# Pieces of the last store, an earlier register load, and three steps moved in a fused attention and MLP kernel

## The chip, the cores and the metric

The kernel runs on one core of one Trainium2 chip. The metric is device time in microseconds for one launch. The core's engines have queues of their own and are named as in the profile: PE (TensorE, matmul), PEld (its weight loads), DVE (VectorE), ACT (ScalarE), POOL (GpSimd) and SP (SyncE, which here does little but issue DMAs and wait). Each engine takes its instructions in program order and waits for others by semaphores.

## The reference

Routing attention with 4 batches, 8 heads, 768 tokens and a head width of 64, followed by an MLP with an ELU between its two products, on 3072 tokens of width 512 with 2048 hidden units:

```python
q_assign = np.argmax(np.einsum('bhsd,hcd->bhsc', q_n, c_n), axis=-1)
k_assign = np.argmax(np.einsum('bhsd,hcd->bhsc', k_n, c_n), axis=-1)
mask = q_assign[:, :, :, None] == k_assign[:, :, None, :]
scores = np.where(mask, scale * np.matmul(q, k.transpose(0, 1, 3, 2)), -1000000000.0)
attn = softmax(scores)
x = np.matmul(attn, v)          # (B,H,S,D) -> (B*S, H*D)
h = x @ w_in
g = np.where(h > 0.0, h, np.exp(np.minimum(h, 0.0)) - 1.0)
out = (g @ w_out).astype(np.float32)
```

Each of q_n, k_n and c_n is its tensor divided by its rows' norms; a query sees only the keys of its own cluster, out of 16 for each head.

## The kernel before

**Attention** (0 to about 331 us) goes through 32 blocks, one for each batch, half of the queries (384) and pair of heads. `slot(n)` works on block n: it multiplies the last block's probabilities with v (`values`, L548), then makes the scores of block n in six steps (`plain`, L510, `masked`, L523), with the exponential on ACT (L532). In odd slots row sums of two blocks come first (`row_sums`, L568). DVE adds up probabilities (L535, L540, L541), and turns raw q and k, loaded in 32 x 32 pieces, into the layout of the matmuls (L715 and near it). POOL later multiplies the results with the reciprocals of the row sums (`scale_x`, L604), two multiplications for two blocks; the reciprocals stand in `r_of` and `e_of`, which are columns of `sums_w`.

All loads of q, k, v and the weights are issued by SP, in program order. `slot_first` is block 0. At its end it asks for the first pair of heads of batch 1's k, for weights, for the second half of q of batch 0 (16 DMAs), and for the second pair of k of batch 1 (four DMAs, `load_k(1, 1)`). `slot(1)` then asks for v of block 2 (`load_v(2)`), `slot(2)` for v of block 3, and so on. There are two buffers for v and two for raw k; the second k buffer is read by the transpose in `slot(3)`.

**The MLP** (331 us to the end) takes the tokens in six groups of 512. Both of its products use a Winograd form of Strassen's scheme, with seven products in place of eight, so there are sums of blocks of x, of the weights and of the hidden values beside the matmuls. Group 0 differs: its first product runs in four calls of `unit(0, u, ...)`, u from 0 to 3, beside the unpacking of the last weights and the sums of blocks of `w_out`.

One `unit` multiplies in the order b1 (a11), b4 (s1), b2 (s2), b1 (a12), b3 (s3), b2 (s4), b3 (a22), each `block_product` being eight matmul instructions of L797. ACT, POOL and DVE make the ELU of four parts: c11 after the fourth product, c12, c22 and c21 later. `elu_exp` is an exponential on ACT (L810) and then a clamp on POOL (L811); `elu` finishes on DVE (L814). L853 and L863 are DVE additions into the banks b2 and b4, which the product with s4, and the parts c22 and after, need. What is left of a unit when its matmuls are issued (`rest_of`: clamp of c21, elu of c12, c22 and c21, a subtraction at L880, and the last of three sums of weights for the next unit, L780 with its DMA) goes into the list `behind`, which `flush_all` issues after the first product of the next unit.

`fill()` is called at four places of a unit. In group 0 it takes one step from the list of weight work. By unit 3 the steps left are three sums of halves of `w_out` (`weight_sum`): 1 (L387), 2 (L389) and 3 (L391), each one DVE addition or subtraction with 2048 elements in a partition; sum 0 (L385) is the last step of unit 2. Sum 2 writes columns of `sums_w` where `r_of` and `e_of` lie. The two multiplications of the last two blocks (`scale_x(last_n - 1, ...)`, `scale_x(last_n, ...)`) are issued between unit 2 and unit 3; the tokens that they write are those of the last group.

`second_product_first` is the second product of group 0: M1 (a11 with b11), M2 (a12 with b21) and M3, then Strassen's form in `chain`. b11 is made of all c11 parts and b21 of all c21 parts; of each of its eight matmul pairs the last two read the part of unit 3.

**The end.** `chain` also does the last group. Its last unit multiplies m6, m2, m7, m3, m4, each eight matmul instructions of L1087, and `take` adds the results into `o_all`: after m2 and before it, columns 0 to 384 of tile 0 and 0 to 256 of tile 1 are there; after m7 and m3 the rest of tile 1; after m4 the last 128 columns of tile 0. The stores of tiles 2 and 3 are issued by SP some products before; those of tiles 1 and 0 by ACT, after m3 and after m4, with 256 KB each. When all is done each engine loads the verdict (`values_load`, L56: an integer in `c["go"]`, made at about 400 us), and branches on it (L57) over `general_path`, which is another form of the whole kernel for inputs that the main form can't do.

Of the kernel before, what the change touches and what calls it, by code (L numbers as in the profile page):

```python
# [30 lines left out]
@with_exitstack  # L31
def kernel(
    ctx: ExitStack,
    tc: tile.TileContext,
    q: bass.AP,
    k: bass.AP,
    v: bass.AP,
    centroids: bass.AP,
    moe_w_in: bass.AP,
    moe_w_out: bass.AP,  # L40
    out: bass.AP,
):
    nc = tc.nc
    ctx.enter_context(nc.allow_non_contiguous_dma(reason="token and weight layouts"))
    keep = ctx.enter_context(tc.tile_pool(name="keep", bufs=1))
    DM, DF = moe_w_in.shape
    c = {
        "ident": keep.tile([P, P], F32, name="ident"),
        "cen": keep.tile([P, q.shape[3]], F32, name="cen"),
        "w_in": keep.tile([P, DM // P, DF], F32, name="w_in"),  # L50
        "w_out": keep.tile([P, DF // P, DM], F32, name="w_out"),
        "ok": keep.tile([P, 4], F32, name="ok"),
        "go": keep.tile([1, 1], I32, name="go"),
    }
    main_path(tc, c, q, k, v, centroids, moe_w_in, moe_w_out, out)
    good = nc.values_load(c["go"][0:1, 0:1], min_val=0, max_val=P)  # L56
    with tc.If(good < P):  # L57
        general_path(tc, c, q, k, v, moe_w_in, moe_w_out, out)


# [1 line left out]
def main_path(ctx, tc, c, q, k, v, centroids, moe_w_in, moe_w_out, out):  # L62
# [569 lines left out]
    def slot_first():  # L632

        for _ in range(6):
            nc.tensor.matmul(
                o_bank, lhsT=blank, rhs=blank[:, 0:1].to_broadcast([P, 512]), start=True, stop=True
            )
        for pr in range(NPR):
            turned(qT[0][pr], first_q[pr], 0)
        nc.tensor.transpose(o_bank[:, :P], work[:, : 2 * D], ident)  # L640
        nc.vector.tensor_copy(cT, o_bank[:, :P])
        clusters_q(0, 0, d_bank)()
        for pr in range(NPR):
            turned(kT[0][pr][:, :CUT], first_k[pr], 0)
        turned(kT[0][0][:, CUT:], first_k[0], CUT // P)
        told = [clusters_k(0, 0, o_bank)]
        flush()
        for pr in range(1, NPR):
            turned(kT[0][pr][:, CUT:], first_k[pr], CUT // P)
        mask_q(0, 0, range(1, 2))  # L650
        first = ring()
        plain(0, 0, first)
        told.append(clusters_k(0, 1, d_bank))
        told[0]()
        flush()
        told[1]()
        load_k(1, 0)
        ask()
        load_q(0, 1)
        load_k(1, 1)  # L660
        for kt in range(NT):
            s = ring() if kt else first
            if kt:
                plain(0, kt, s)
            masked(0, kt, s)
            exponential(kt, s)
            if kt == 2:
                flush()
            elif kt == 3:
                sums_begin()  # L670


    def slot(n):
        b, at = n // NB, n % NB
        more = b + 1 < B
        sums_of = n - 2 if n > 1 and n % 2 else None
        pair_done = n - 4 if n >= 4 and n % 2 == 0 else None
        if sums_of is not None:
            row_sums(sums_of)
            take_sums(sums_of)  # L680
        flush(powers)
        if n > 0:
            values(n - 1)
        told = None
        if at == (1 if b else 3):
            told = clusters_q(b, 1, d_bank)
        elif at == 5 and more:
            told = clusters_q(b + 1, 0, d_bank)
        elif at in (6, 7) and more:
            told = clusters_k(b + 1, at - 6, d_bank)  # L690
        if n > 0:
            sums_end(n - 1)
        if pair_done is not None:
            nc.gpsimd.tensor_copy(mark, summed[(n - 1) % 2][:, :1])
            scale_x(n - 4, r_of)
            scale_x(n - 3, e_of)
        if n > 0:
            take_values(n - 1)
        if told is not None:
            told()  # L700
        if sums_of is not None:
            reciprocals(sums_of)
            spread(sums_of)

        if n + 1 < len(blocks):
            load_v(n + 1)
        if at == 0 and b:
            nc.vector.transpose(qT_all[1], raw_q_all)
        if at == 1 and b and more:
            load_q(b + 1, 0)  # L710
        if at == 0 and more:
            load_k(b + 1, 0)
            load_k(b + 1, 1)
        elif 2 <= at < 6 and more:
            nc.vector.transpose(kT[(b + 1) % 2][at - 2], raw_k[at % 2])  # L715
            if n == 2:
                nc.vector.transpose(qT_all[1], raw_q_all)
                load_q(1, 0)
            if at < 4:
                load_k(b + 1, at)  # L720
            elif at == 4:
                nc.vector.transpose(qT_all[0], raw_q_all)
                load_q(b + 1, 1)
        weigh(n)

        for kt in range(NT):
            s = ring()
            plain(n, kt, s)
            masked(n, kt, s)
            exponential(kt, s)  # L730
            if kt == 3:
                sums_begin()
        flush(later)
# [92 lines left out]
    def unit(k_, u, after_second=None, fill=None):  # L826

        fill = fill or (lambda: None)
        x11, t3, x21, x22 = x_parts(k_)
        t1, t2, t4 = x_s  # L830
        a11, a12, s1, a22 = w_parts(u)
        s2, s3, s4 = (w_tmp[:, m] for m in range(3))
        b1, b2, b3, b4 = sets[(k_ + u) % 2]
        m5, u3 = stage[:, 0], stage[:, 1]
        low, high = slice(2 * u, 2 * u + 2), slice(FC // 2 + 2 * u, FC // 2 + 2 * u + 2)
        c11, c12 = g[:, low, :QS], g[:, low, QS:]
        c21, c22 = g[:, high, :QS], g[:, high, QS:]

        block_product(b1, a11, x11, True)
        nc.scalar.copy(b2, b1)  # L840
        flush_all()
        yield
        block_product(b4, s1, t1, True)
        nc.scalar.copy(m5, b4)
        if after_second is not None:
            after_second()
        if k_ == 1 and u == 3:
            for _ in slots_w:
                fetch()
        yield  # L850
        block_product(b2, s2, t2, False)
        nc.scalar.copy(b3, b2)
        nc.vector.tensor_tensor(b2, b2, m5, op=Alu.add)  # L853
        fill()
        fill()
        if u < 3:
            w_step(k_, u + 1, 0)
        block_product(b1, a12, x21, False)
        elu_exp(c11, b1)
        block_product(b3, s3, t3, False)  # L860
        nc.scalar.copy(u3, b3)
        elu(c11, b1)
        nc.vector.tensor_tensor(b4, b4, u3, op=Alu.add)  # L863
        if k_ > 0:
            for t in {2: ("t1",), 3: ("t2", "t3", "t4")}.get(u, ()):
                t_step(0, t)
        fill()
        block_product(b2, s4, x22, False)
        if u < 3:
            w_step(k_, u + 1, 1)  # L870
        elu_exp(c12, b2)
        elu_exp(c22, b4)
        fill()
        block_product(b3, a22, t4, False)

        def rest_of():
            elu_exp(c21, b3)
            elu(c12, b2)
            elu(c22, b4)
            nc.vector.tensor_tensor(c12, c22, c12, op=Alu.subtract)  # L880
            elu(c21, b3)
            if u < 3:
                w_step(k_, u + 1, 2)

        behind.append(rest_of)
# [367 lines left out]
    def chain(units):  # L1253
# [6 lines left out]
        for i, u in enumerate(units):  # L1260
# [14 lines left out]
            u.product("m2")  # L1275
            u.take(0)
            u.note("m2")
            if nxt:
                seven_first(nxt)
            u.product("m7")  # L1280
# [9 lines left out]
            u.product("m3")  # L1290
            u.take(1)
            if ending:
                store_tile(u.k_, 1, nc.scalar)
            u.product("m4")
            if nxt:
                nxt.t("t4")
            u.note("m4")
        if ending:
            u.take(2)
            store_tile(u.k_, 0, nc.scalar)  # L1300
        elif u.of == "in":
            u.take(2)
        else:
# [116 lines left out]
        elif m == "M4":  # L1420
            store(k_, 0)

    def store_tile(k_, tile_, by):
        n = 4 * k_ + tile_
        at, t = n // HT, n % HT
        by.dma_start(
            out[at * HS : (at + 1) * HS].rearrange("(p t) m -> p t m", t=HT)[:, t],
            o_all[:, tile_],
        )

    def store(k_, tiles):
# [121 lines left out]
    def early_on():  # L1553
        while steps:
            weigh_step(*steps.pop(0))
            flush()

    blanks(0)
    for u in range(4):
        if u == 1:  # L1560
            blanks(1)
        run(unit(0, u, finish_attention if u == 0 else None, fill_weights))
        if u == 1:
            findings()
        elif u == 2:
            scale_x(last_n - 1, r_of)
            scale_x(last_n, e_of)
    second_product_first(early_on)

    table = table_rest()  # L1570
# [276 lines left out]
```

## Time and profile before

Three runs took 888.82, 889.41 and 889.57 us; the median is 889.41.

| | before |
|---|---|
| profiled execution | 889.5 us |
| its span, first to last instruction | 887.7 us |
| granted TensorE clock | 0.998 |
| PE busy | 876.6 us, 99% |
| DVE busy | 710.7 us, 80% |
| ACT busy | 447.0 us, 50% |
| POOL busy | 227.3 us, 26% |
| DMA, mean over the span | 164 GB/s |

The profile is one execution. In a timeline a line has the start and the time of an instruction or of several alike in us, the engine, the line of the code, what is written and read, and in brackets the idle time of the engine before it with what ended that. A matmul in f32 is two instructions of the trace. Ends of matmuls are modelled, so distances between starts are the surer measure. Shares of busy time are means over stages that differ: attention, the first group and the others.

### The profile page before, as it was taken

To read this page: it belongs to the slowest core of one execution; us is meant where nothing else is said; L and a number is where in the kernel's file an instruction comes from. 1 tells how busy PE (TensorE), PEld (TensorE's weight loads), DVE (VectorE), ACT (ScalarE), POOL (GpSimd) and SP (SyncE) were. 2 spreads that over 40 slices of the span, in tenths; PEclk is the share of its full clock that TensorE was granted. 3 is DMA by queue.
4 is the path that set the end of the run, shared out by engine and by line. 5 is a ranking of instruction groups with operands and counts; after the bars stand their busy time and mean duration, and the time that the engine had idled before them with its cause. 6 is when DMAs were issued, how large, how long until landed. Compare 5 with 4: busy or idle time off the path is not lost.

```text
span 887.7 us, 17035 instructions
## 1 busy us (share of the span) xinstructions
PE 876.6 (99%) x6437; PEld 677.6 (76%) x6441; DVE 710.7 (80%) x1041; ACT 447.0 (50%) x853; POOL 227.3 (26%) x293
## 2 busy tenths in 40 slices
PE   8999999999999999999999999999999999999997
PEld 5444444444444448899989999999999999999997
DVE  4789998999988997897688957884788568956784
ACT  6667786787868754412243235422642364225421
POOL 0011121121113555841323013511351035102300
PEclk9999999999999999999999999999999999999999
DMA  7766685366337441165677876286618661876172
GB/s 219 185 127 175 158 181 121 123 125 159 84 107 217 129 141 62 59 148 151 206 249 245 276 212 178 52 279 207 188 48 265 217 191 42 267 205 205 49 231 82
DMA packets 157369, 145.68 MB, mean 164 GB/s; under 512 B 89824, under 2 KB 109280, under 8 KB 156256
## 3 DMA queue, kind: packets, MB, share of 16 engines
q1 hardware_dynamic: 151584, 132.45, 51.0%
q0 software_dynamic: 5408, 11.54, 5.7%
q8 instruction: 53, 0.87, 0.4%
q10 hardware_dynamic: 288, 0.52, 0.2%
q14 instruction: 36, 0.29, 0.1%
HBM read 114.59 MB, written 21.50 MB: 153 GB/s over the span
## 4 chain that ended last, share of the span: by engine, by line
PE 92%; POOL 3%; issue 2%; DVE 1%; DMA 1%; ACT 0%; SPq 0%; POOLq 0%; ACTq 0%
PE bank L1087 23%; PE o_bank L548 15%; PE banks L510 14%; PE bank L797 12%; PE bank L1177 9%; PE o_bank L1087 4%; PE banks L523 3%; PE o_bank L797 2%; PE d_bank L1087 2%; PE o_bank L1177 2%; PE d_bank L568 1%; PE d_bank L438 1%; POOL kq_g L811 1%; PE d_bank L1177 1%; PE banks L616 1%
## 5 line engine op out<-in xcount | busy, mean ns | idle before, releaser
L532 ACT ACTIVATE p_out<-banks 128x768 f32<-128x768 f32 x192 | 154.1, 811 | 25.2 <-PE banks L523 24.2
L548 PE MATMUL o_bank<-p_out,kq_g 128*64 128x384 f32 x768 | 130.9, 490 | 0.7 <-DMA kq_g<-in_v_dram 0.7
L548 PEld LDWEIGHTS o_bank<-p_out,kq_g 128*64 128x64 f32 x768 | 52.3, 137 | 75.5 <-issue 69.8
L811 POOL TENSOR_SCALAR kq_g<-kq_g 128x512 f32<-128x512 f32 x96 | 69.0, 728 | 109.7 <-ACT kq_g L810 108.3
L535 DVE TENSOR_TENSOR sums_w<-p_out 128x1536 f32<-128x1536 f32 x32 | 59.1, 1846 | 10.1 <-ACT p_out L532 10.1
L810 ACT ACTIVATE kq_g<-bank 128x512 f32<-128x512 f32 x68 | 39.8, 602 | 38.5 <-PE bank L797 18.4
L797 PE MATMUL bank<-xT,spare 128*128 128x256 f32 x256 | 59.2, 379 | 0.0
L540 DVE TENSOR_TENSOR sums_w<-sums_w,p_out 128x1536 f32<-128x1536 f32 x32 | 56.2, 1757 | 3.3 <-DVE sums_w L535 0.5
L609 POOL DMA_DIRECT2D sums_w<-xT x28 | 17.7, 649 | 154.3 <-DVE xT L585 92.0
L1087 PE MATMUL bank<-w_out,kq_g 128*128 128x128 f32 x448 | 56.0, 275 | 0.3 <-DVE kq_g L814 0.3
L1087 PEld LDWEIGHTS bank<-w_out,kq_g 128*128 128x128 f32 x448 | 53.4, 192 | 0.8 <-DVE kq_g L814 0.5
L797 PEld LDWEIGHTS bank<-xT,spare 128*128 128x128 f32 x256 | 48.3, 190 | 6.4
L797 PE MATMUL bank<-x_sum,w_in 128*128 128x256 f32 x224 | 52.9, 379 | 0.0
L814 DVE SCALAR_TENSOR_TENSOR kq_g<-kq_g,bank 128x512 f32<-128x512 f32 x68 | 44.9, 679 | 7.7 <-POOL kq_g L811 7.7
L797 PEld LDWEIGHTS bank<-x_sum,w_in 128*128 128x128 f32 x224 | 42.6, 190 | 5.8
L1195 POOL TENSOR_TENSOR spare<-x_sum 128x128 f32<-128x128 f32 x16 | 7.3, 457 | 154.4 <-PE bank L1177 88.8
L1391 DVE TENSOR_TENSOR kq_g<-kq_g 128x1024 f32<-128x1024 f32 x36 | 43.8, 1219 | 0.0
L562 ACT ACTIVATE xT<-o_bank 128x384 f32<-128x384 f32 x32 | 15.6, 489 | 53.8 <-PE o_bank L548 53.8
L604 POOL TENSOR_TENSOR xT<-xT,sums_w 128x384 f32<-128x384 f32 x32 | 41.1, 1305 | 1.6 <-DMA sums_w<-xT 1.6
L510 PE MATMUL banks<-x_sum,xT 64*128 64x384 f32 x192 | 39.8, 492 | 0.0
L510 PE MATMUL banks<-kq_g,xT 64*128 64x384 f32 x192 | 39.6, 491 | 0.0
L510 PE MATMUL banks<-x_sum,kq_g 64*128 64x384 f32 x192 | 39.6, 491 | 0.0
(379 smaller groups left out, 2026.6 us busy)
## 6 DMA issues: line engine op xcount, KB each, us to landing
kq_g<-in_v_dram SPq DMA_DIRECT2D x32, 384.0 KB, 3.7
sums_w<-far_s_s SPq DMA_DIRECT2D x42, 256.0 KB, 3.7
spare<-w_far SPq DMA_DIRECT2D x32, 256.0 KB, 3.0
words_w<-far_s_s SPq DMA_DIRECT2D x26, 256.0 KB, 3.2
out_dram<-p_out SPq DMA_DIRECT2D x22, 256.0 KB, 3.3
w_out<-in_q_dram SPq DMA_DIRECT2D x112, 48.0 KB, 2.6
sums_w<-xT POOLq DMA_DIRECT2D x28, 192.0 KB, 3.2
sums_w<-far_s_q SPq DMA_DIRECT2D x21, 256.0 KB, 3.6
```

What stands on the lines that cost most here:

```text
L510: nc.tensor.matmul(s[:, e, :HS], lhsT=kT[b % 2][pr][rows, ts(kt, P)], rhs=qT[half][pr][rows], start=True, stop=False,)
L532: nc.scalar.activation(probs[kt], s[:, :, :HS], Act.Exp, scale=SCALE)
L535: nc.vector.tensor_tensor(add_to, probs_all[:, : 4 * HS], probs_all[:, 4 * HS : 8 * HS], op=Alu.add)
L540: nc.vector.tensor_tensor(add_to, add_to, probs_all[:, 8 * HS :], op=Alu.add)
L548: nc.tensor.matmul(o_bank[64 * e : 64 * e + 64, :HS], lhsT=v_raw[n % 2][:, e, kt], rhs=probs[kt][:, e], start=(kt == 0), stop=(kt == NT - 1),)
L604: nc.gpsimd.tensor_tensor(x_of(n), x_of(n), r, op=Alu.mult)
L797: nc.tensor.matmul(bank[:, ts(f, QS)], lhsT=left[:, ch, ts(f, P)], rhs=right[:, ch], start=first and f == 0 and ch == 0, stop=ch == 1, ski ...
L811: nc.gpsimd.tensor_scalar(to, to, 1.0, 0.0, op0=Alu.min, op1=Alu.max)
L814: nc.vector.scalar_tensor_tensor(to, to, -1.0, as_part(bank, to), op0=Alu.add, op1=Alu.max)
L1087: nc.tensor.matmul(bank[:, :P], lhsT=left[:, f], rhs=right[:, f], start=first and f == 0, stop=last and f == 3, skip_group_check=True,)
L1177: nc.tensor.matmul(bank[:, ts(f, P)], lhsT=left[:, ts(f, P)], rhs=right, start=m in ("m1", "m5") and f == 0, stop=True, skip_group_check=True,
L1391: nc.vector.tensor_tensor(b[to][:, f], b[x][:, f], b[y][:, f], op=op)
```

## The change

The stores of the last two tiles become four: two by SP after m2, with the columns that are complete by then (384 of tile 0, 256 of tile 1), and two by ACT after m3 and m4 with the other columns (256 of tile 1, 128 of tile 0). The load of the verdict into registers, on every engine, moves from the end to the place behind the two SP stores, between m2 and m7 of the last unit; the branch stays at the end. `load_k(1, 1)` moves from the end of `slot_first` behind `load_v(2)` in `slot(1)`. In unit 3 of group 0 one call of `fill()` moves behind the addition L863, which puts `weight_sum(2)` there. The two multiplications between units 2 and 3 move into unit 3, behind its second product, and so behind the `flush_all` there.

```diff
-    good = nc.values_load(c["go"][0:1, 0:1], min_val=0, max_val=P)
-    with tc.If(good < P):
+    with tc.If(c["good"] < P):
...
         load_q(0, 1)
-        load_k(1, 1)
...
         if n + 1 < len(blocks):
             load_v(n + 1)
+        if n == 1:
+            load_k(1, 1)
...
         nc.vector.tensor_tensor(b2, b2, m5, op=Alu.add)
         fill()
-        fill()
+        if k_ or u < 3:
+            fill()
...
         fill()
+        if not k_ and u == 3:
+            fill()
         block_product(b2, s4, x22, False)
...
             u.note("m2")
+            if ending:
+                store_tile(u.k_, 0, nc.sync, slice(0, 3 * P))
+                store_tile(u.k_, 1, nc.sync, slice(0, 2 * P))
+                c["good"] = nc.values_load(c["go"][0:1, 0:1], min_val=0, max_val=P)
             if nxt:
                 seven_first(nxt)
             u.product("m7")
...
             if ending:
-                store_tile(u.k_, 1, nc.scalar)
+                store_tile(u.k_, 1, nc.scalar, slice(2 * P, DM))
             u.product("m4")
...
             u.take(2)
-            store_tile(u.k_, 0, nc.scalar)
+            store_tile(u.k_, 0, nc.scalar, slice(3 * P, DM))
...
+    def last_scaled():
+        scale_x(last_n - 1, r_of)
+        scale_x(last_n, e_of)
...
-        run(unit(0, u, finish_attention if u == 0 else None, fill_weights))
+        run(unit(0, u, {0: finish_attention, 3: last_scaled}.get(u), fill_weights))
         if u == 1:
             findings()
-        elif u == 2:
-            scale_x(last_n - 1, r_of)
-            scale_x(last_n, e_of)
```

`store_tile` takes the columns as a further argument, and stores `o_all[:, tile_, cols]` into the same columns of the output rows.

More of the change, by code (lines that the diff above doesn't have):

```diff
@@ L1421, in taken, with store_tile @@
             store(k_, 0)
-    def store_tile(k_, tile_, by):
+    def store_tile(k_, tile_, by, cols=slice(0, DM)):
         n = 4 * k_ + tile_
@@ L1426, in store_tile @@
         by.dma_start(
-            out[at * HS : (at + 1) * HS].rearrange("(p t) m -> p t m", t=HT)[:, t],
-            o_all[:, tile_],
+            out[at * HS : (at + 1) * HS].rearrange("(p t) m -> p t m", t=HT)[:, t, cols],
+            o_all[:, tile_, cols],
         )
```

## The prediction

> **What bounds the kernel.** I read the page's busy table first, then the idle column of the matmul groups, then the timelines of the places found there. The busy table says TensorE:
>
> ```profile
> PE 876.6 (99%) x6437; PEld 677.6 (76%) x6441; DVE 710.7 (80%) x1041; ACT 447.0 (50%) x853; POOL 227.3 (26%) x293
> ```
>
> So the end moves only where TensorE waits, and behind its last matmul. The timeline of TensorE shows three waits after the start-up:
>
> ```profile
> 42.92 4.09 PE L548 MATMUL o_bank<-p_out,kq_g 128*64 128x384 f32 x24 [0.69 <-DMA kq_g<-in_v_dram]
> 378.23 1.97 PE L797 MATMUL o_bank<-xT,spare 128*128 128x256 f32 x8 [0.31 <-DVE o_bank L853]
> 383.54 7.86 PE L1087 MATMUL bank<-w_out,kq_g 128*128 128x128 f32 x68 [0.28 <-DVE kq_g L814]
> ```
>
> Matmul ends are modelled, so I price a wait by starts. Values elsewhere begin 0.42 us after the last row-sum matmul (41.74): due at 42.16, came at 42.92, **0.76**. The eight L797 matmuls from 376.03 come every 0.216: due 377.76, **0.47**. Twelve L1087 matmuls from 381.76 come every 0.112: due 383.10, **0.45**. With 0.07 of smaller slips after these, 0.99 us is lost between 376 and 389. After 390 no gap between matmul starts is over 0.11 us beyond its usual pitch until 881.3. The change aims at these three and the tail.
>
> **v before k.** SyncE's queue issues in order:
>
> ```profile
> 35.31 2.73 SPq L174 DMA_DIRECT2D w_out<-in_k_dram  x4
> 38.14 1.11 SPq L190 DMA_DIRECT2D kq_g<-in_v_dram  x2
> ```
>
> The first of the two v loads is the one waited for: issued 38.14, landed 42.88, so 4.74 us. With the four k issues behind it, it goes out at about 35.3 and lands at 40.1 even at that slow rate, 2.1 us before 42.16. The four k issues start 0.6 later, at 35.9, and land near 42; their reader, the transpose of that k (L715), runs at 51.35. The next v load and the q loads behind keep their times. Nothing else is late there: the last exponential of the slot ends at 42.36 and is needed by the sixth step of values, some 2.7 us after 42.16. One cover thins: at 58.30 a transpose waits 0.34 for k data, whose time is set by SyncE and does not move up with TensorE; but VectorE idles 1.00 us for TensorE at 67.64, so it catches up. Gain **0.76**. Even at 5.94 us, the slowest v load after the start (59.74 to 65.68), it lands at 41.3; only the 7.7 us of the start, with some ten loads in flight, would come too late, so the bounds are 0 and 0.76.
>
> **The scalings and the weight sum.** GpSimd and VectorE around unit 3 of the first group:
>
> ```profile
> 370.42 3.38 POOL L811 TENSOR_SCALAR kq_g<-kq_g 128x512 f32<-128x512 f32 x2
> 373.77 2.40 POOL L604 TENSOR_TENSOR xT<-xT,sums_w 128x384 f32<-128x384 f32 x2
> 376.14 0.61 POOL L811 TENSOR_SCALAR kq_g<-kq_g 128x512 f32<-128x512 f32 x1
> 376.72 1.27 POOL L780 TENSOR_TENSOR spare<-w_in,spare 128x512 f32<-128x512 f32 x1
> 378.91 1.83 POOL L811 TENSOR_SCALAR kq_g<-kq_g 128x512 f32<-128x512 f32 x1
> ...
> 377.39 0.69 DVE L853 TENSOR_TENSOR o_bank<-o_bank,spare 128x512 f32<-128x512 f32 x1
> 377.99 2.28 DVE L387 TENSOR_TENSOR p_out<-w_out 128x2048 f32<-128x2048 f32 x1
> 380.31 2.58 DVE L389 TENSOR_TENSOR sums_w<-w_out,p_out 128x2048 f32<-128x2048 f32 x1
> 382.81 0.68 DVE L814 SCALAR_TENSOR_TENSOR kq_g<-kq_g,bank 128x512 f32<-128x512 f32 x1
> ```
>
> Before, the two scalings (L604) hold back unit 2's last clamp (L811) by 2.4 us, with it the elu at 376.79, L853, and TensorE. And c11's elu at 382.81 stands behind two weight sums. Afterwards GpSimd runs clamp, L780, its DMA, the two scalings, then c11's clamp.
>
> Here a rule must be set against a row. The Trainium skill, "SBUF — State Buffer", section "Who interferes with whom", says that GpSimd and a VectorE operation with two SBUF inputs exclude each other for the whole instruction, whoever starts first. It speaks against this move, which puts the scalings beside L387. By the scaling's row (1.00 us when it runs freely at 373.77) the pair would be done at 378.5 and c11's clamp at 379.1. The trace sides with the rule: the clamp that starts at 378.91 beside L387 takes 1.83, not 0.61, ending 0.47 after L387 does. I take the lock. The page's warning that GpSimd's DMA issue is starved too I leave aside: it is told of other VectorE modes, and the issue at 378.29 beside L387 took its usual 0.59.
>
> Step by step: clamp 373.8 to 374.4; L780 to 375.6; VectorE's subtraction L880, wanted at 374.56, waits for it and ends at 376.2; elu to 376.8; **L853 to 377.4**, in time for 377.76, so the 0.47 goes. GpSimd's DMA issue to 376.5, first scaling to 377.5. L387 then holds the port to 379.75; second scaling to 380.55 and c11's clamp to 381.1. VectorE, with L389 moved behind, idles some 1.4 us from 379.75, and c11's elu ends at 381.8. TensorE, now 0.56 earlier, needs it at 381.21 + 1.34 = 382.55: the 0.45 goes too.
>
> What is late next is c21, the last clamp-and-elu of the unit. Before it ended 6.0 us after c11's elu began (382.81 to 388.81); now L389 lies in between, 2.5 us more: 381.15 + 8.5 = 389.65. TensorE reaches it after the first product (64 x 0.1116 = 7.14) and 12 matmuls: 381.21 + 7.14 + 1.34 = 389.69. Add a semaphore's 0.1 and a wait of about 0.15 remains. VectorE's later work there is about 1 us later against TensorE, but it idles 0.81 and 1.80 us for TensorE at 400.49 and 406.05, which absorbs it. Gain 0.99 - 0.15 = **0.84** (bounds 0.3 and 0.99). Without the lock it would be 0.99.
>
> **The tail.** After the last matmul (starts to 881.04) come an addition, ScalarE's last store at 881.68, its landing, and SyncE's closing chain, 1.95 us from landing 885.75 to 887.7.
>
> ```profile
> L56 SPq TENSOR_LOAD <-go x1: 1120/1120/1120, 401.8 to 401.8; - x1
> L56 PEldq TENSOR_LOAD <-go x1: 597/597/597, 880.0 to 880.0; - x1
> L57 SPq COMPARE_BRANCH  x1: 50/50/50, 878.9 to 878.9; - x1
> L57 PEldq COMPARE_BRANCH  x1: 4402/4402/4402, 880.7 to 880.7; - x1
> DMA to landing us min/median/max: 2.1/3.4/4.3
> ```
>
> The loads' durations are in ns. The last store took 4.07 us to land; 14 of its 16 completions came by 883.74, 2.1 us after issue. The two late ones fall where the instruction queues fetch 16 and 8 KB for the branch, 881.7 to 884.1.
>
> *Verdict load.* TensorE's sequencer is ahead of its matmuls by only some 0.26 us at the new place (its wait for m7's weights is stamped 878.10, m7 starts at 878.37). Load 0.60 plus 0.1 to the next dispatch leave TensorE idle 0.45; m7, m3, m4 queue behind it, so the last store goes out at 882.15. Bounds 0 (it ran 1.2 us ahead at the old place) and 0.75; I take 0.45, the nearer row. Its branch hardly moves: the sequencer catches up to 880.65, so the return stays at 885.07. VectorE (0.81 us) and ScalarE (0.48) load in idle time. SyncE's load now follows two more stores: it ends at 881.0, and its branch goes from 878.9 to 881.4. Its own return took 3.2 us (878.91 to 882.12), so it is back at 884.6; its closing chain needs 2.2 us: 886.8. That is the new floor.
>
> *Smaller last stores.* 64 KB instead of 256. The skill's "DMA: Bandwidth & Descriptors", in its breakdown of the fixed cost, has about 2 us fixed plus bytes at 436 GB/s: the piece would save 192 KB / 436 = 0.44 us (an estimate from that page), which the load's 0.45 eats: tail 0. The trace shows the landing set by two congested engines, which on the last two stores drain 16 rows of 2 KB at 0.08 us from 884.1 to 885.3. With 1 KB and 512 B rows I estimate half of that, 0.7 us less: landing near 885.05. That, plus 1.95, gives 887.0 to 887.2, behind the floor: gain **0.55**. Bounds -0.4 (load paid, stragglers unchanged) and 0.9 (the floor).
>
> **Sum.** The profiled execution took 889.5, of which 887.7 is span; 1.8 lies around it and stays. 889.5 - 0.76 - 0.84 - 0.55 = 887.35. The median of the runs shown is 889.41, 0.1 lower, so **887.3**, 0.24% less. A measurement of this kernel tells from no change about 0.2%, here 1.78 us: faster means below 887.6.
>
> **Rivals.**
> *Tail pays nothing.* The page's fixed cost holds, or SyncE's late branch fetch joins the three others and returns about 0.5 later. For it: TensorE's branch took 4.4 us where SyncE's took 3.2. Against: the 2.1 us of the uncongested completions. 889.4 - 1.6 = 887.8; with the load fully paid 888.2. Chance 0.24.
> *The second product waits for c21.* VectorE's order puts 8.5 us behind c11's elu, and my margin is nil: each 0.1 us later on GpSimd is 0.1 us of TensorE. With 0.6 us more 0.25 is left of this part: 887.9. Chance 0.13.
> *Slower.* The same place, if the scalings lose the port badly. A pair beside VectorE sums at 329.70 took 3.73 us. Begun at 379.75 they would end at 383.5, c11's clamp at 384.1, c21's elu at 392.6: a wait of 3.0 us, this part -2.0, the time 890.1. It decides once c11's clamp ends after 383.2, 2.1 us past my sum. Against: with L389 moved behind, VectorE has no sum to run then. Chance 0.08.
> *As summed*, 0.55; own range 886.6 to 887.9.
>
> **Numbers.** The first case is faster in 85% of its weight, the tail's in 30%, c21's in 45%: 0.47 + 0.07 + 0.06 = 0.60. Slower 0.07, from the last rival. Same 0.33. The range 886.5 to 888.5 takes in the gains' upper bounds (0.76 + 0.99 + 0.9) and the middle rivals, and leaves the slow one out.
>
> **What would show it.** Values at slot 3 with no DMA wait. L853 ending before its product is due. VectorE idle about 1.4 us ahead of c11's elu, released by L811, and a TensorE wait under 0.3 us some 8.5 us later. A TensorE gap near 0.45 between the last unit's m2 and m7. The last landing under 3 us from issue, and SyncE's branch at about 2.5 us later than before. Wrong: a c21 wait near 1 us, no gap at m7, or a last landing still past 4 us.

## The result, and the profile after

The changed kernel took 886.52 us (median; 885.86 to 887.09), the kernel before, beside it on the same chip, 888.97 us. The ratio is 0.9974, 95% interval 0.9964 to 0.9983: **0.26% faster**. Forecast were 887.3 us and 2.15 us gained; the gain is 2.3 to 2.5 us. A second set of runs gave 886.52 us again, with 0.9978 (0.9969 to 0.9987). The profiled execution took 886.62 us, its span is 884.8 (before 887.7).

Line numbers have moved a little: values are L547 now, the scalings L603, the weight sums 1 to 3 L386, L388 and L390, the addition L863 is L864, the matmuls of the end L1090, the branch L56, and the load stands in L1284.

The page's busy row hardly moves, since TensorE is the bound before and after:

```profile
PE 876.3 (99%) x6437; PEld 677.6 (77%) x6441; DVE 712.6 (81%) x1041; ACT 447.0 (51%) x853; POOL 227.9 (26%) x293
```

**v before k.** The timeline of SyncE's queue and of TensorE around slot 3 (start, time, engine, line, operation):

```profile
35.79 0.56 SPq L189 DMA_DIRECT2D kq_g<-in_v_dram  x1
36.39 3.12 SPq L173 DMA_DIRECT2D w_out<-in_k_dram  x4
39.61 0.59 SPq L189 DMA_DIRECT2D kq_g<-in_v_dram  x1
...
42.13 2.16 PE L547 MATMUL o_bank<-p_out,kq_g 128*64 128x384 f32 x12
```

v goes out ahead of the four k loads and lands at 39.67. Values start at 42.13, 0.79 us earlier, with no bracket behind the row: TensorE waits for nothing there.

**The scalings and the weight sum.** TensorE's timeline in the last unit of the first product and in the first of the second:

```profile
376.97 1.89 PE L797 MATMUL o_bank<-xT,spare 128*128 128x256 f32 x8
378.69 1.89 PE L797 MATMUL bank<-x_sum,w_in 128*128 128x256 f32 x8
380.42 9.38 PE L1090 MATMUL bank<-w_out,kq_g 128*128 128x128 f32 x80
389.63 1.95 PE L1090 MATMUL o_bank<-w_out,kq_g 128*128 128x128 f32 x16
```

The product with s4 and the second product's first 80 matmuls now run through: both waits there are gone. But 80 matmuls at a pitch of 0.1116 us would have the next row at 389.35, and it comes at 389.63. So a wait of 0.28 is left inside M2, ahead of the pairs that read c21. The timeline of GpSimd and VectorE shows where it comes from:

```profile
375.73 1.96 POOL L603 TENSOR_TENSOR xT<-xT,sums_w 128x384 f32<-128x384 f32 x2
375.89 0.69 DVE L853 TENSOR_TENSOR o_bank<-o_bank,spare 128x512 f32<-128x512 f32 x1
376.49 3.42 DVE L386 TENSOR_TENSOR p_out<-w_out 128x2048 f32<-128x2048 f32 x1
377.66 3.29 POOL L811 TENSOR_SCALAR kq_g<-kq_g 128x512 f32<-128x512 f32 x2
...
380.41 0.69 DVE L814 SCALAR_TENSOR_TENSOR kq_g<-kq_g,bank 128x512 f32<-128x512 f32 x1 [0.50 <-POOL kq_g L811]
...
381.61 2.28 DVE L388 TENSOR_TENSOR sums_w<-w_out,p_out 128x2048 f32<-128x2048 f32 x1
...
383.81 2.70 DVE L390 TENSOR_TENSOR words_w<-w_out,p_out 128x2048 f32<-128x2048 f32 x1
```

The two scalings run back to back in 1.96 us, and the weight sum L386 beside them takes 3.42 us where it took 2.28. c11's clamp (the first of the two in the row of L811) then stands behind that sum. c11's elu starts at 380.41; sums L388 and L390 come behind it, and c21's elu, the last of the part, only at 388.35.

**The tail.** The register loads and the branch, from the views of these two lines (durations in ns, then first and last start in us):

```profile
L1284 PEldq TENSOR_LOAD <-go x1: 491/491/491, 874.9 to 874.9; - x1
L1284 SPq TENSOR_LOAD <-go x1: 760/760/760, 878.3 to 878.3; - x1
```

```profile
L56 SPq EVENT_SEMAPHORE  x8: 17/17/17, 882.6 to 883.1; - x8
...
L56 PEldq COMPARE_BRANCH  x1: 4515/4515/4515, 878.4 to 878.4; - x1
L56 SPq COMPARE_BRANCH  x1: 50/50/50, 879.5 to 879.5; - x1
```

TensorE's queue does its load at 874.9, while m7's matmuls start at 876.87; no gap between starts in the last five products is over 0.15 us. SyncE branches at 879.46 and is back at 882.57, 3.1 us later; its closing chain of 2.2 us ends the kernel at 884.8. The last landing, at 882.86, comes 2.78 us behind its issue (before 4.07), and 14 of its 16 completions by 882.11; SyncE comes to the wait for it at 882.97, so the landing alone would have let the kernel end only 0.1 us earlier. From the start of the last matmul to the end it is 5.35 us, before 6.69.

### The profile page after: what moved, and what is told of

Its sections match the earlier page's. It is cut to its first block, busy times and chain, and to the rows that moved or that the text cites. A ratio compares the mean times of both kernels' runs of the same rounds, so it can differ in the third digit from the quotient of the medians.

```text
span 884.8 us, 17038 instructions
## 1 busy us (share of the span) xinstructions
PE 876.3 (99%) x6437; PEld 677.6 (77%) x6441; DVE 712.6 (81%) x1041; ACT 447.0 (51%) x853; POOL 227.9 (26%) x293
## 4 chain that ended last, share of the span: by engine, by line
PE 98%; DMA 1%; DVE 0%; SPq 0%; issue 0%; ACT 0%
PE bank L1090 24%; PE bank L797 16%; PE banks L509 15%; PE o_bank L547 15%; PE bank L1180 9%; PE o_bank L1090 4%; PE banks L522 4%; PE o_bank L797 3%; PE d_bank L1090 2%; PE o_bank L1180 2%; PE d_bank L567 1%; PE d_bank L437 1%; PE d_bank L1180 1%; PE d_bank L797 1%; PE banks L615 1%; DMA p_out<-in_q_dram 1%
## 5 line engine op out<-in xcount | busy, mean ns | idle before, releaser
L547 PE MATMUL o_bank<-p_out,kq_g 128*64 128x384 f32 x768 | 130.9, 490 | 0.0
L547 PEld LDWEIGHTS o_bank<-p_out,kq_g 128*64 128x64 f32 x768 | 52.3, 137 | 74.8 <-issue 70.8
L811 POOL TENSOR_SCALAR kq_g<-kq_g 128x512 f32<-128x512 f32 x96 | 70.0, 739 | 109.5 <-ACT kq_g L810 108.2
L1090 PE MATMUL bank<-w_out,kq_g 128*128 128x128 f32 x448 | 56.0, 275 | 0.0
L1090 PEld LDWEIGHTS bank<-w_out,kq_g 128*128 128x128 f32 x448 | 53.4, 192 | 0.5 <-DVE kq_g L814 0.2
L603 POOL TENSOR_TENSOR xT<-xT,sums_w 128x384 f32<-128x384 f32 x32 | 40.6, 1292 | 1.6 <-DMA sums_w<-xT 1.6
L509 PE MATMUL banks<-kq_g 64*128 64x384 f32 x192 | 39.6, 491 | 0.0
```

Source lines behind the costliest of these rows:

```text
L509: nc.tensor.matmul(s[:, e, :HS], lhsT=kT[b % 2][pr][rows, ts(kt, P)], rhs=qT[half][pr][rows], start=True, stop=False,)
L547: nc.tensor.matmul(o_bank[64 * e : 64 * e + 64, :HS], lhsT=v_raw[n % 2][:, e, kt], rhs=probs[kt][:, e], start=(kt == 0), stop=(kt == NT - 1),)
L603: nc.gpsimd.tensor_tensor(x_of(n), x_of(n), r, op=Alu.mult)
L811: nc.gpsimd.tensor_scalar(to, to, 1.0, 0.0, op0=Alu.min, op1=Alu.max)
L1090: nc.tensor.matmul(bank[:, :P], lhsT=left[:, f], rhs=right[:, f], start=first and f == 0, stop=last and f == 3, skip_group_check=True,)
```

## The experiments

Start-up differs by up to a microsecond between executions, so two distances are compared: **body**, from the start of values in slot 3 to the start of the last matmul, and **tail**, from there to the end. Body leaves out the wait for v. Ratios are to the kernel before on the same chip, with their 95% intervals; the first row has the medians of the kernel before beside the others. A kernel with a single run is read by its profile alone, its time settles nothing.

| kernel | median us (runs) | ratio | body | tail |
|---|---|---|---|---|
| before | 888.2 to 889.0 | 1 | 838.12 | 6.69 |
| changed | 886.52 (11) | 0.9974 (0.9964, 0.9983) | 837.31 | 5.35 |
| changed, again | 886.52 (11) | 0.9978 (0.9969, 0.9987) | 837.32 | 5.48 |
| tail part alone | 887.54 (12) | 0.9992 (0.9983, 1.0) | 838.12 | 5.30 |
| other parts alone | 887.55 (21) | 0.9989 (0.9983, 0.9996) | 837.31 | 5.88 |
| verdict loaded last | 886.70 (14) | 0.9980 (0.9972, 0.9989) | 837.32 | 6.21 |
| whole tiles | 886.69 (17) | 0.9979 (0.9972, 0.9986) | 837.32 | 5.48 |
| six more loads | 889.90 (1) | - | 840.88 | 5.12 |
| scalings undone | 887.28 (1) | - | 837.58 | 5.27 |
| weight sum undone | 887.66 (1) | - | 838.54 | 5.35 |
| third sum behind | 885.95 (12) | 0.9976 (0.9967, 0.9985) | 837.02 | 5.26 |
| no scalings | 886.07 (1) | - | 837.02 | 5.29 |
| hint | 886.55 (20) | 0.9981 (0.9974, 0.9988) | 837.60 | 4.81 |
| hint and third sum behind | 885.93 (7) | 0.9973 (0.9962, 0.9984) | 837.33 | 5.16 |

The edits below are against the changed kernel.

### The tail part alone

```diff
+        load_k(1, 1)
...
-        if n == 1:
-            load_k(1, 1)
...
-        if k_ or u < 3:
-            fill()
+        fill()
...
-        if not k_ and u == 3:
-            fill()
...
-        run(unit(0, u, {0: finish_attention, 3: last_scaled}.get(u), fill_weights))
+        run(unit(0, u, finish_attention if u == 0 else None, fill_weights))
...
+        elif u == 2:
+            last_scaled()
```

> The changed kernel with the three moves of v, of the weight sum and of the scalings undone; only the end is changed (four stores in pieces, verdict loaded between m2 and m7). If the parts add up: the last matmul starts near 881.0 us as before (the three waits of 0.76, 0.47 and 0.45 us are back), and from that start to the end of the span it is 5.4 us as in the changed kernel, not 6.7 us as before. The time is then 1.3 us under the kernel before. If the gain at the end is an accident of one execution, the distance is anywhere between 5.4 and 6.7 us.

Body is back at 838.12, as before, and the tail is 5.30, as in the changed kernel: the two halves of the change don't touch each other. One thing was not expected: with v again behind k, values started at 41.32 without a wait. In this execution TensorE ran 0.84 us earlier there than in the profile of before, v was issued 1.04 us earlier (37.10), landed at 41.09 after 3.98 us, and was in time. **The wait for v is not in every execution**: of the two profiles with the old order of loads, one has all of it and one has none.

### The verdict loaded at the end, and the tiles stored whole

```diff
+    c["good"] = nc.values_load(c["go"][0:1, 0:1], min_val=0, max_val=P)
     with tc.If(c["good"] < P):
...
-                c["good"] = nc.values_load(c["go"][0:1, 0:1], min_val=0, max_val=P)
```

> The changed kernel with the verdict loaded at the end again, behind the last store; the stores stay in pieces. My prediction's theory (the early load stops TensorE for 0.45 us): the last matmul starts 0.45 us earlier than in the changed kernel. Theory now (TensorE's sequencer runs some 2 us ahead of the matmuls, the load costs nothing there): the last matmul starts at the same 879.4 us, and the end comes 0.1 to 0.5 us later, since TensorE, VectorE and ScalarE branch 0.5 to 0.8 us later, return later, and their code fetches lie further into the last store.

Body is unchanged (837.32), so the early load costs TensorE nothing: the prediction's 0.45 us falls. The tail of this profile is 6.21, with the last store 3.74 us on its way, but the profiled execution (887.51 us) lies 0.8 above the median of its kernel, which is only 0.2 above the changed kernel's.

```diff
-                store_tile(u.k_, 0, nc.sync, slice(0, 3 * P))
-                store_tile(u.k_, 1, nc.sync, slice(0, 2 * P))
...
-                store_tile(u.k_, 1, nc.scalar, slice(2 * P, DM))
+                store_tile(u.k_, 1, nc.scalar, slice(0, DM))
...
-            store_tile(u.k_, 0, nc.scalar, slice(3 * P, DM))
+            store_tile(u.k_, 0, nc.scalar)
```

> The changed kernel with tiles 1 and 0 stored whole by ScalarE again, 256 KB each; the verdict is loaded early. Theory now (the size of the last stores sets their landing beside the code fetches): the last store lands 3.5 to 4.1 us after its issue, not 2.8 us, SyncE is back from its branch before that, and the end comes 0.6 to 1.3 us later than in the changed kernel. [...]

A miss: the two stores of 256 KB land 2.69 and 2.87 us behind their issue, not 3.5 to 4.1, and the time is 886.69. And in the kernel above, with the verdict loaded last, the two small pieces took 4.45 and 3.74 us. In these profiles it isn't the size that made the last landing late.

### Six more loads on TensorE

```diff
                 c["good"] = nc.values_load(c["go"][0:1, 0:1], min_val=0, max_val=P)
+                for _ in range(6):
+                    nc.values_load(c["go"][0:1, 0:1], engines=[mybir.EngineType.PE], min_val=0, max_val=P)
```

> The changed kernel with six further loads of the verdict on TensorE alone, behind the one between m2 and m7. Each takes 0.5 us, and with its bounds check some 0.6 to 0.9 us of the sequencer, 3.6 to 5.4 us in all. Theory now (the sequencer is 2.0 us ahead at this place): TensorE idles 1.6 to 3.4 us ahead of m7. The prediction's theory (0.26 us ahead): it idles 3.3 to 5.1 us, so the idle time is the loads' total less the lead, and the lead is read from the difference.

TensorE's timeline:

```profile
875.98 1.06 PE L1090 MATMUL bank<-w_out,kq_g 128*128 128x128 f32 x8
880.38 1.13 PE L1090 MATMUL bank<-sums_w,p_out 128*128 128x128 f32 x8 [3.34 <-issue]
```

Now m7 waits, and for "issue": nothing but its own queue. By the raw records the seven loads hold the queue from 874.89 to 880.27, 5.38 us; the last matmul of m2 starts at 876.76, so m7 is 3.50 us late. The difference, **1.9 us, is how far the queue is ahead** of the matmuls at that place. The one load of the changed kernel holds the queue for 0.6 us and disappears in it.

### The other parts alone, and the changed kernel again

```diff
+    c["good"] = nc.values_load(c["go"][0:1, 0:1], min_val=0, max_val=P)
     with tc.If(c["good"] < P):
...
-            if ending:
-                store_tile(u.k_, 0, nc.sync, slice(0, 3 * P))
-                store_tile(u.k_, 1, nc.sync, slice(0, 2 * P))
-                c["good"] = nc.values_load(c["go"][0:1, 0:1], min_val=0, max_val=P)
...
-                store_tile(u.k_, 1, nc.scalar, slice(2 * P, DM))
+                store_tile(u.k_, 1, nc.scalar, slice(0, DM))
...
-            store_tile(u.k_, 0, nc.scalar, slice(3 * P, DM))
+            store_tile(u.k_, 0, nc.scalar)
```

> The changed kernel once more, for comparison with the next runs on the same chip. 2.0 to 2.5 us under the kernel before; v of block 2 lands at least 1.5 us ahead of its use and TensorE does not wait for it, as in the other profiles with v ahead of k.

> The changed kernel with the end as it was before: tiles 1 and 0 stored whole, verdict loaded last. The first run with whole tiles and the one with a late verdict each came within 0.3 us of the changed kernel in their medians. Theory: either part alone frees the end of the collision of store rows and code fetches, so that the two parts do not add up; without both, the end is 0.9 to 1.3 us later than in the changed kernel (from the last matmul 6.3 to 6.7 us). Rival: the shorter end was the luck of single profiles; then it is at most 0.4 us later.

On one chip, 887.55 without the tail part and 886.52 with it: by the medians the tail part is worth 1.0 us. The two kernels above, each with one half of the tail part, are only 0.2 us slower by their medians (886.70 and 886.69), at most 0.5 by their ratios. **By the medians either half gives most of the gain; they do not add.** This compares runs on two chips, on which the kernel before took 888.60 and 888.63; the intervals of the ratios overlap (0.9972 to 0.9989 against 0.9983 to 0.9996). With the verdict loaded last the final landing took 4.07, 3.74 and 3.26 us (the kernel before, verdict loaded last, other parts alone); with it early, 2.23 to 2.87 us in all eleven profiles. But the pieces alone are as fast in the median as the early load alone, though their one profile has a late landing. Nor is it simply that the first 16 KB of instructions for the branch are fetched earlier: this fetch starts 0.64 to 0.82 us behind the last matmul in the three profiles with the late landings, but also 0.81 behind it in the kernel without scalings (below), whose last store landed after 2.81. Why the early load makes the landing shorter, and which of the landings and the engines' returns sets the end in a typical execution without it, stays open.

### The scalings undone, and the weight sum undone

```diff
-        run(unit(0, u, {0: finish_attention, 3: last_scaled}.get(u), fill_weights))
+        run(unit(0, u, finish_attention if u == 0 else None, fill_weights))
...
+        elif u == 2:
+            last_scaled()
```

> The changed kernel with the two scalings back between units 2 and 3; the weight sum stays behind L864. The clamp of c21 waits for the scalings, L853 comes late, and TensorE waits 0.47 us ahead of the product with s4 as before; the wait for c11 (0.45) is gone, c21's elu ends some 0.5 us ahead of its need, so there is no wait for it. First matmul of M2 to last of M1 together: 0.2 us later than in the changed kernel against the start of unit 3.

TensorE waits again for L853, as it did before, and nowhere else in the two stages:

```profile
377.91 1.97 PE L797 MATMUL o_bank<-xT,spare 128*128 128x256 f32 x8 [0.31 <-DVE o_bank L853]
```

By starts that is 0.47, with 0.07 of small slips; the 0.28 at c21 is gone. 0.47 + 0.07 - 0.28 = 0.26, and body is 0.27 longer.

```diff
-        if k_ or u < 3:
-            fill()
+        fill()
...
-        if not k_ and u == 3:
-            fill()
```

> The changed kernel with the weight sum back ahead of c11's elu; the scalings stay inside unit 3. GpSimd keeps the port through both scalings, so L386 takes 3.4 us, and the next sum follows it: c11's elu ends near 383.1 us where TensorE needs it at 381.8, a wait of about 1.3 us in M1; the s4 product has none; c21 is in time. In all 0.9 to 1.1 us later than in the changed kernel: the moved scalings alone are worse than nothing, and the two moves need each other. Rival (the port changes hands after each instruction, as I predicted): L386 takes 2.3 us and the second scaling waits, a wait near 0.9 us.

GpSimd, VectorE and TensorE of this kernel:

```profile
376.36 3.42 DVE L386 TENSOR_TENSOR p_out<-w_out 128x2048 f32<-128x2048 f32 x1
377.52 5.34 POOL L811 TENSOR_SCALAR kq_g<-kq_g 128x512 f32<-128x512 f32 x2
...
379.87 2.52 DVE L388 TENSOR_TENSOR sums_w<-w_out,p_out 128x2048 f32<-128x2048 f32 x1
...
382.32 0.67 DVE L814 SCALAR_TENSOR_TENSOR kq_g<-kq_g,bank 128x512 f32<-128x512 f32 x1
```

```profile
380.30 1.50 PE L1087 MATMUL bank<-w_out,kq_g 128*128 128x128 f32 x12
383.05 1.16 PE L1087 MATMUL bank<-w_out,kq_g 128*128 128x128 f32 x8 [1.25 <-DVE kq_g L814]
```

With two sums in a row on VectorE, c11's elu comes at 382.32 and M1 waits: the matmul starts lie 1.52 us apart, 1.41 over the pitch. Body is 1.23 longer than the changed kernel's and **0.42 longer than before**. So moving the scalings alone would have lost 0.42, moving the sum alone gained 0.54, and both together gain 0.81.

### The third sum behind the flush, and no scalings

```diff
-        if not k_ and u == 3:
-            fill()
         block_product(b2, s4, x22, False)
...
-        fill()
+        if k_ or u < 3:
+            fill()
         block_product(b3, a22, t4, False)
```

With these two calls gone from unit 3, the third sum stays in the list, and the loop that empties it issues it in the flush of the second product. The edit without scalings has `pass` as the body of `last_scaled`.

> The changed kernel with the third of the last unit's weight sums (2.70 us on VectorE in the profile after) moved from ahead of the two flush multiplications into the flush's gap. Theory (the 0.28 us that TensorE now waits ahead of c21 in the last group's first unit comes from that sum standing in VectorE's order ahead of c21's elu): the wait goes, the last matmul starts 0.28 us earlier against the start of the first group's fourth unit (837.31 us now, 837.03 then), unless the sum's own reader, the last unit's weights, comes due first: then a new wait of up to 1 us stands ahead of the last unit. Rival (the wait comes from GpSimd's clamp of c21, which is late by itself): it stays at 0.2 to 0.3 us.

> Leaves out part of the computation: the last two multiplications of attention results by the reciprocals of their row sums are not made. Theory (GpSimd's two multiplications, back to back, keep the shared port, and the first weight sum on VectorE takes 3.42 us for 2.28 because of it): the sum takes 2.28 us, the elu of c11 runs 1.1 to 1.9 us earlier, the wait ahead of c21 goes (0.28 us), and the last matmul starts 0.28 us earlier against the fourth unit. Rival (the sum is long because of the transfers or TensorE's writes beside it): it stays near 3.4 us and the wait stays.

TensorE of the first and of the second:

```profile
380.75 9.09 PE L1089 MATMUL bank<-w_out,kq_g 128*128 128x128 f32 x80
389.68 1.95 PE L1089 MATMUL o_bank<-w_out,kq_g 128*128 128x128 f32 x16
```

```profile
376.35 2.40 DVE L386 TENSOR_TENSOR p_out<-w_out 128x2048 f32<-128x2048 f32 x1
...
378.68 0.67 DVE L814 SCALAR_TENSOR_TENSOR kq_g<-kq_g,bank 128x512 f32<-128x512 f32 x1
```

```profile
380.29 9.09 PE L1090 MATMUL bank<-w_out,kq_g 128*128 128x128 f32 x80
389.22 1.95 PE L1090 MATMUL o_bank<-w_out,kq_g 128*128 128x128 f32 x16
```

In both, 80 matmuls take 8.93 us of starts, which is their pitch: the wait at c21 is gone and body is 0.29 shorter. No new wait takes its place in the first: the weights that hang on the moved sum are not late for TensorE. So it is VectorE's chain behind c11 that was 0.28 late, and either of two steps mends it. The second leaves out the two scalings, and so prices the port that GpSimd and VectorE share: without the scalings beside it L386 takes 2.40 us for 3.42, so **the lock costs VectorE 1.0 us**, and c11's elu starts 1.6 us earlier (378.68 to 380.41, less 0.13 of start-up). In the changed kernel L386 ends 2.21 us after the second scaling, about the 2.28 that it takes undisturbed: it stood still until both were done. The ratio of the first, 0.9976, can't be told from the changed kernel's 0.9974 and 0.9978: 0.29 us is 0.03%.

### A hint on the branch, and both together

```diff
+    tc.mark_branch_hint_location("general", "LikelyTaken", engines=mybir.ALL_ENGINES)
-    with tc.If(c["good"] < P):
+    with tc.If(c["good"] < P, label="general"):
```

> The changed kernel with a hint at the program's head that the branch over the repair path is likely taken, for every engine. Theory (the end hangs on SyncE, whose next instructions are fetched only once its branch is decided: 3.1 us from the branch to its next instruction, and the fetches land the last stores late): SyncE is back 0.3 to 0.5 us behind its branch at 879.5, the last two stores land 1.6 to 2.0 us behind their issue, and the end hangs on the last landing: last matmul to end 4.2 to 4.8 us in place of 5.35 to 5.5, a time 0.6 to 1.2 us below that of the changed kernel. Rival (the hint doesn't bring the instructions in ahead, or only costs its own issue): SyncE takes 3.1 us again, the time is the same or up to 1 us longer.

The view of the branch's line (here L57) in the kernel with the hint:

```profile
L57 SPq EVENT_SEMAPHORE  x8: 17/17/17, 880.1 to 882.7; - x8
...
L57 PEldq COMPARE_BRANCH  x1: 402/402/402, 878.5 to 878.5; - x1
L57 SPq COMPARE_BRANCH  x1: 70/70/70, 879.6 to 879.6; - x1
```

The mechanism holds: SyncE is back 0.52 us behind its branch instead of 3.1, TensorE's branch takes 0.4 instead of 4.5. The end then hangs on the last landing, 882.52 (2.34 us behind its issue, not the 1.6 to 2.0 expected), and the tail is 4.81, 0.54 to 0.67 shorter. Yet the median is 886.55: no gain (the profiled execution itself took 886.14). Part of it is given back in the body, 0.29 us, at one new wait of TensorE:

```profile
811.58 0.57 ACT L1269 COPY bank<-bank 128x512 f32<-128x512 f32 x1 [0.82 <-PE bank L1181]
...
812.25 0.91 PE L1181 MATMUL bank<-spare,sums_w 128*128 128x128 f32 x6 [0.16 <-issue]
```

ScalarE's copy, which in the changed kernel waits 0.53 for its bank, starts 0.30 later against it, and TensorE, which is to write that bank next, is 0.33 late.

> The changed kernel with both: the third weight sum behind the flush, and the hint on the branch. Theory (each takes a step off the path, one after the other: 0.28 us ahead of the last matmul, as the profile of the first shows, and 0.55 to 0.65 us behind it, as the profile of the second shows): last matmul 837.02 us behind the start of the first group's fourth unit, last matmul to end 4.8 us, a ratio to the kernel before of 0.9965 to 0.9970, which is 0.6 to 0.9 us below the changed kernel's 0.9974 to 0.9978. Rival (a profiled end says nothing of an unprofiled one here: the time of the hint alone was no lower than the changed kernel's): a ratio of 0.9974 to 0.9980.

A miss as well. Body is 837.33 and not 837.02, because the same wait of 0.33 is there again (at 811.5), and the tail is 5.16: SyncE is back at 879.77, but the last landing takes 2.69 us, to 882.54. The ratio 0.9973 is that of the changed kernel. No kernel tried here beats the changed one by more than a measurement can tell.

## Why the prediction was right, and where it was not

Forecast and result agree to 0.8 us, but only just within the range of 886.5 to 888.5, and below the 886.6 to 887.9 given for the sum itself. 0.4 of the miss is the anchor: 889.41 was the median of three runs, where larger sets gave 888.2 to 889.0. That the gain, 2.15 against 2.0 to 2.5, came out so well is in part luck: the tail was priced 0.4 too low and v probably too high, and the two errors cancel.

- **v before k: right in mechanism, probably too large.** 0.76 was forecast, and in the profiled pair values start 0.79 earlier. But the row of 0.69 was one execution's. The tail part alone ran its profile without that wait. By the ratios, the other parts alone gain 0.98 us, of which 0.81 is body: 0.2 for v. From the other side, the changed kernel gains 1.2 to 1.6 over the tail part alone, which leaves 0.4 to 0.8 for v. The first of these is good to some 0.6 us and the second to some 1.2, so the times can't tell v's part from nothing, nor from all of 0.76. One reading was wrong besides: 5.94 us was not the slowest v load after the start, since the same profile has 7.62 us (issued at 73.07) and 9.08 (at 274.73); a load that slow would have come too late here as well.
- **Scalings and weight sum: right.** 0.84 forecast, 0.81 measured. L853 ended at 376.6, as worked out (377.4 less 0.79). The forecast that the two moves need each other was only implied; the two undone versions show it. Two details went otherwise: VectorE's idle time ahead of c11's elu is 0.50, not 1.4, because GpSimd's scalings ran as a pair and L386 paid for the port (3.42 us), not the second scaling. The elu ended at 381.1 all the same, where the 381.8 forecast less 0.79 is 381.0. And the wait at c21 is 0.28, not 0.15.
- **The rule on the port: right as a price, with the order assumed wrongly.** The Trainium skill, "SBUF — State Buffer", section "Who interferes with whom", has the pair belong to whoever starts first, for the whole instruction. The trace agrees that it is held, and adds that two instructions in a row kept it: L386, expected to get it between the two scalings, started 0.76 us after the first of them and did not. The lock's 1.0 us is there (2.40 without the scalings), and without it body would be 0.29 shorter.
- **The verdict load: wrong. This is the failed step.** "TensorE's sequencer is ahead of its matmuls by only some 0.26 us at the new place" took the wait stamped 878.10 for m7's; it belongs to m3, whose matmuls start at 879.37. (A stamp is the start of what the queue itself executes, a load or a wait. In the changed kernel TensorE's queue has three there, the load at 874.88, a wait at 875.48 and one at 876.50. The load was put ahead of m7, so the first of the two waits is m7's; the kernel before has the same two at 876.49 and 878.10. With six more loads they stand at 880.27 and 880.40, and m7 starts between them, at 880.38.) The queue is 1.9 us ahead, as six more loads show, and the load costs nothing: no gap at m7, which the prediction itself had named as a sign of being wrong. Without the 0.45 its sum would have the last landing at 884.6 and the end at the floor, 886.8, so a tail gain of 0.9 instead of 0.55. The tail part measured 1.0 to 1.1 by the medians, 0.7 to 1.0 by the ratios.
- **The floor from SyncE's return: right in mechanism, 0.4 us too late.** It is the step that set the end in the profile after: branch at 879.46, back after 3.1, chain of 2.2. Products and stores come 1.60 us earlier there than in the profile before; with this added back, the branch is at 881.06 (forecast 881.4), the return at 884.17 (884.6) and the end at 886.4 (886.8). From the last matmul the forecast comes to 5.3 us and 5.35 were measured, but that is luck: it counts from a last matmul put 0.45 too late.
- **Smaller last stores: not borne out.** Neither the 0.44 us estimated for the bytes from the Trainium skill, "DMA: Bandwidth & Descriptors", section "Anatomy of one DMA — SWDGE (gpsimd) path", nor the 0.7 that I estimated from the rows: whole tiles land in 2.7 to 2.9 us too, and cost 0.2 us more by the median, within the noise. That section fits its sum to DMAs issued by GpSimd, which the prediction did not say; these stores are ScalarE's. The last landing did come below 3 us, as forecast, though with whole tiles it does as well; with the early load all profiles have it there.

Of the rivals, "tail pays nothing" falls with the tail's 0.7 to 1.1 us, "waits for c21" holds at 0.28 and no more, and "slower" did not come, though with the scalings moved alone body would have been 0.42 longer.

## What to carry to other kernels

Find out how far an engine's queue is ahead of its work before you price an instruction that only the queue executes: match the stamps of waits to their instructions, or fill the queue with more of the same and see when the engine starts to idle. A wait that one profile shows may be missing from the next execution; price it from several. Two moves that look like separate edits may be one: here one alone loses 0.4 us, the other alone gains 0.5, and together they gain 0.8.

## What the hardware showed that was not expected

- GpSimd kept the shared port over two instructions in a row (1.96 us), and VectorE's sum beside them stretched from 2.40 to 3.42 us.
- The branch over the other form of the kernel cost SyncE 3.1 us until its next instruction; with a hint at the program's head 0.52 us. In both kernels with the hint, 812 us on, ScalarE started one copy 0.30 us late and TensorE waited 0.33; it is in none of the other profiles. What links the two is open.
- A load of a register on TensorE's queue took 0.30 to 0.63 us, with what follows it 0.6 to 1.0, and one of them was free where the queue was 1.9 us ahead.
